# Linear attention and Fourier mixing on one core: keys and own query tiles turned by block transposes on DVE in place of TensorE transposes

## Chip, cores and metric

The kernel runs on one core of one Trainium2 chip. The metric is the device time of one execution in microseconds (us). The engines are named as the profile names them: PE is TensorE, PEld its weight loads, DVE is VectorE, ACT is ScalarE, POOL is GpSimd, SP is SyncE, which issues nearly all DMAs here.

## The reference

Eight batches of 576 tokens, 8 heads of 64 columns (512 columns in all), float32. First a linear attention: softmax of each query over its 64 columns, softmax of each key column over the 576 tokens, a 64x64 product of keys and values for each head, and queries times that product. Then a Fourier mixing over tokens and columns, a layer norm, and two dense layers with a relu between.

```python
q_s = exp(q - max(q, axis=-1));  q_s = q_s / (sum(q_s, axis=-1) + 1e-9)
k_s = exp(k - max(k, axis=2));   k_s = k_s / (sum(k_s, axis=2) + 1e-9)
kv  = einsum('bhsd,bhse->bhde', k_s, v)
x   = einsum('bhsd,bhde->bhse', q_s, kv)          # then laid out as (8, 576, 512)
u   = x + real(fft(fft(x, axis=1), axis=2))
un  = (u - mean(u)) / sqrt(var(u) + 1e-6)         # w_ch1: 512x2048, w_ch2: 2048x512
out = u + relu(un @ w_ch1) @ w_ch2
```

Keys arrive transposed: `kT[b]` is 512 rows (head and column) by 576 tokens. Queries and values arrive as 576 tokens by 512 columns.

## The kernel before

One class, `_Block`, holds all steps as small functions. The main function gives each step a planned time, sorts all steps by it, and issues them in that order; each engine runs its own instructions in the order written. From the second stage on the planned unit is 0.87 us (`scale = 0.87`). So the plan sets only the order on each engine. What sets the real start is the engine itself and its waits.

The work is staged by group of 512 token rows. In stage `order` (1 to 8) PE runs the two dense layers of one group (`up`, 56 units, then `deep_down` or `down`), both as Strassen schemes of seven products over three PSUM banks, `ba`, `bb` and `bc`. The weights stream from HBM in chunks through four places of `big` (`load`, L454); a chunk is asked for when the one four before it is used up (`used`). Between the products of one Strassen step DVE reads a bank and adds a temporary (L1216, L1257 in the up part, L1380 in the down part), and the product after next writes the same bank again.

Into the same stage the attention of batch `b = order + 1` is woven by `attention_timed`, then its folding (`folded`), its Fourier products (`block`, `mix_own`, `mix_shared`) and the norm of the next group. `attention_timed` serves batches 2 to 7. Batch 0 is done in the opening by a list of times written by hand, batch 1 beside the first group's dense layers. Both keep their own steps, of which `first_keys` and the `q_` functions matter here.

For one batch `attention_timed` plans:

- Four key rows `r` (128 rows of `kT`, that is two heads, by 576 tokens). `keys_to` (L642) and `values_to` (L649, L650) load them. `k_exp` takes the maximum along the tokens on DVE (L666), the exponential on ACT with that maximum as its bias and the sum as a second output (L672), and inverts the sum on DVE (L677, L678). `k_turn` transposes four blocks of 128 tokens on PE into PSUM (L690), copies them to SBUF on ACT (L696), then the last block of 128 tokens (L700), of which DVE keeps 64 (L704). `k_times_v` multiplies by the values in five steps (L716) and scales the two diagonal 64x64 blocks by the inverse sum into `kvr` (L724).
- Four own query tiles of 128 tokens. `q_load` (L736) loads one; `q_exp` takes the maximum of each head (L760), eight exponentials of 64 columns with that maximum as bias (L766), sums and inverts on DVE (L785 to L787) and, for two tiles of four, multiplies (L796). `q_turn` transposes four blocks on PE (L824) and copies them out on ACT (L834), for two tiles with the tokens reversed. `q_times_kv` multiplies by `kvr` (L886) and writes the tile, on DVE with the scale (L901) or on ACT without (L903).
- In even batches a tile of tokens shared by two batches, the `t_` functions, which stay on PE.

`ahead(b + 1)` places the first loads of the next batch into the current stage. A float32 product is two PE instructions, each with a weight load; a transpose is one. Waits between engines are set by the tiles that they share: a tile from a pool with n buffers (`bufs=n`) waits for its reader n uses before.

Of the kernel before, what the change touches and what calls it, by code (L numbers as in the profile page):

```python
# [46 lines left out]
P = 128  # L47
B, H, S, DH = 8, 8, 576, 64
D = H * DH
# [11 lines left out]
NT = Q // 2 + 1  # L61
KT = D // P
NF = FF // P
GT = 4 * P
# [72 lines left out]
class _Block:  # L137
    def __init__(self, ctx, tc, q, kT, v, w1, w2, ft, cd, out):
# [14 lines left out]
        for b in range(2):  # L153
            t = c.tile([P, NR, P], F32, name=f"kvr{b}")
            nc.gpsimd.memset(t[:], 0.0)
            self.kvr.append(t)
# [14 lines left out]
        for t in self.kss[:2]:  # L171
            nc.gpsimd.memset(t[0:64, 4, :], 0.0)

# [63 lines left out]
    def warm(self, n):  # L237

        t = self.ps.tile([P, 512], F32, tag="ba", name="ba")
        for _ in range(n):  # L240
            self.nc.tensor.matmul(t[:, 0:2 * P], lhsT=self.ident[:], rhs=self.kvr[1][:, 0:2, :], start=True, stop=True)

# [235 lines left out]
    def attention_timed(self, b, start, end):  # L478

        keys = [("k", b, r) for r in range(NR)]  # L480
        tail = [("t", b)] if b % 2 == 0 else []
        own = [("q", b, c, u) for c, u in ((0, 0), (0, 1), (1, 1), (1, 0))]
        first = start + 14 + 5 * len(tail)
        gap, steps = (end - 13.7 - first) / 3, []
        places = [first + gap * i for i in range(4)]
        shared = start + 14
        if tail and start == 0:
            shared, places = 17, [14, 21, 26, 31.3]
        for i, it in enumerate(keys):
            t = start + 3.5 * i  # L490
            if i > 1:
                steps += at(t - 5, self.k_load(it)[:1]) + at(t + 1.8, self.k_load(it)[1:])
            steps += at(t, self.k_exp(it)) + at(t + 4, self.k_turn(it)) + at(t + 7, self.k_times_v(it))
# [5 lines left out]
        loads = [(t, self.q_load(it)) for t, it in zip(places, own)] + [(shared - 6, self.t_load(it)) for it in tail]  # L499
        loads.sort(key=lambda s: s[0])  # L500
        for t, load in loads[2:]:
            steps += at(t - 6, load)
        return steps + at((33 if start < 0 else 39) if tail else 22, self.t_times_kv(b))

    def ahead(self, b):


        steps = [(20 + r, lambda r=r: self.keys_to(b, r)) for r in range(3)]
        steps += [(35 + r, lambda r=r: self.values_to(b, r)) for r in range(2)]
        q = [self.q_load(("q", b, 0, u)) for u in range(2)]  # L510
# [121 lines left out]

    def k_load(self, it):
        _, b, r = it
        if r < 2:
            return []
        steps = [] if r < 3 else [(0, lambda: self.keys_to(b, r))]
        return (steps or [(0, lambda: None)]) + [(0, lambda: self.values_to(b, r))]

    def keys_to(self, b, r):  # L640
        k = self.work.tile([P, S], F32, tag="k", name="k", bufs=3)[:]
        self.nc.sync.dma_start(k, self.kT[b, r * P:(r + 1) * P, :])  # L642
        self.live["k", b, r] = [k]

    def values_to(self, b, r):
        nc = self.nc
        cols = slice(r * P, (r + 1) * P)
        v = self.work.tile([P, NC, P], F32, tag="v", name="v", bufs=2)
        nc.sync.dma_start(v[:, 0:4, :], self.v[b, 0:512, cols].rearrange("(c p) n -> p c n", p=P))  # L649
        nc.sync.dma_start(v[:, 4, :], self.v[b, S - P:, cols])  # L650
        self.live["k", b, r].insert(1, v)

    def spare(self, n):
# [5 lines left out]
        return t  # L659

    def k_exp(self, it):
        nc, V, live = self.nc, self.nc.vector, self.live

        def top():
            m = self.small.tile([P, 1], F32, tag="km", name="km", bufs=3)
            V.reduce_max(m[:], live[it][0], axis=AX.X, negate=True)  # L666
            live[it].append(m)

        def exp():
            k, m = live[it][0], live[it].pop()  # L670
            rec = self.small.tile([P, 1], F32, tag="krec", name="krec", bufs=8)
            nc.scalar.activation(k, k, ACT.Exp, bias=m[:, 0:1], accum_out=rec[:, 0:1])  # L672
            live[it].append(rec)

        def inverse():
            rec = live[it][2]
            V.tensor_scalar(out=rec[:], in0=rec[:], scalar1=ATT_EPS, scalar2=None, op0=ALU.add)  # L677
            V.reciprocal(rec[:], rec[:])  # L678

        return [(0, top), (0.8, exp), (4.5, inverse)]  # L680

    def k_turn(self, it):
        nc, live = self.nc, self.live
        box = []

        def turn():
            k = live[it][0]
            pt = self.turned()
            for c in range(4):
                nc.tensor.transpose(pt[:, c, :], k[:, c * P:(c + 1) * P], self.ident[:])  # L690
            box.append(pt)

        place = lambda: self.kss[it[2] % 2]

        def four():
            nc.scalar.copy(place()[:, 0:4, :], box.pop(0)[:])  # L696

        def last():
            pt = self.turned()
            nc.tensor.transpose(pt[:, 0, :], live[it][0][:, S - P:], self.ident[:])  # L700
            box.append(pt)

        def fifth():
            nc.vector.tensor_copy(place()[64:, 4, :], box.pop(0)[64:, 0, :])  # L704
            live[it].append(place())

        return [(0, turn), (0.7, four), (0.7, last), (1.2, fifth)]

    def k_times_v(self, it):
        nc, live, (_, b, r) = self.nc, self.live, it  # L710

        def times():
            _, v, rec, ks = live.pop(it)
            pk = self.acc((P, P))
            for c in range(NC):
                nc.tensor.matmul(pk, lhsT=ks[:, c, :], rhs=v[:, c, :], start=(c == 0), stop=(c == NC - 1))  # L716
            live[it] = pk, rec

        def scale():
            pk, rec = live.pop(it)  # L720
            for h in range(2):
                s = slice(64 * h, 64 * h + 64)
                to = self.kvr[b % 2][s, r, s]
                nc.vector.tensor_scalar(out=to, in0=pk[s, s], scalar1=rec[s, 0:1], scalar2=None, op0=ALU.mult)  # L724

        return [(0, times), (1.7, scale)]

# [99 lines left out]
    def q_turn(self, it):  # L827
        _, b, c, u = it
        box = []

        def copy():
            pt = box.pop()
            qT = self.work.tile([P, NR, P], F32, tag="qT", name="qT", bufs=2)
            self.nc.scalar.copy(qT[:], pt[:] if c == u else pt[:, :, ::-1])  # L834
            self.live[it][0] = qT

        return [(0, lambda: box.append(self.turned_q(it))), (0.8, copy)]
# [31 lines left out]
    def q_times_kv(self, it):  # L869
# [10 lines left out]
        def times():  # L880
            qT, *rec = self.live.pop(it)
            px = self.acc((P, D))
            box.insert(0, px)
            box.extend(rec)
            for r in range(NR):
                nc.tensor.matmul(px[:, r * P:(r + 1) * P], lhsT=qT[:, r, :], rhs=self.kvr[b % 2][:, r, :], start=True,  # L886
                                 stop=True)
# [19 lines left out]
    def t_times_kv(self, b):  # L907
# [5 lines left out]
        def times():  # L913
            px = self.acc((P, D))
            for r in range(NR):
                nc.tensor.matmul(px[:, r * P:(r + 1) * P], lhsT=self.F[:, 2 * r + j], rhs=kvr[:, r, :], start=True,
                                 stop=True)
            box.append(px)
# [617 lines left out]
def kernel(ctx: ExitStack, tc: tile.TileContext, q, kT, v, w1, w2, ft,  # L1536
# [149 lines left out]
```

## Time and profile before

| what | value |
|---|---|
| median of 3 runs | 1069.19 us (1068.7 to 1069.22) |
| span of the profiled execution | 1068.4 us, 16964 instructions |
| PE granted clock, mean | 1.000 |
| DMA | 236.04 MB, mean 221 GB/s |
| PE key transposes, L690 and L700 | x96 and x24, 273 ns each |
| PE query transposes, L824 from `q` | x124, 273 ns each |
| PE key products, L716 | x240, 275 ns each |
| ACT query exponentials, L766 | x216, 338 ns each |
| stage of batch 4 (529 to 644 us): PE, DVE, ACT, POOL busy | 115.0, 74.8, 43.1, 52.3 us |

The span runs from the first to the last instruction of one profiled execution; the time of a run takes in what lies around it. No separate time is recorded for the profiled execution. PE's instructions are pipelined, so the 273 ns of one are longer than the distance to the next. A group's line gives the engine, the operation, output and inputs by tile, the shape, the count, the busy time and the mean time of one; then the idle time of the engine before them and what ended it. A line of the order of time gives start and length in us.

### The profile page before, as it was taken

To read this page: it belongs to the slowest core of one execution; us is meant where nothing else is said; L and a number is where in the kernel's file an instruction comes from. 1 tells how busy PE (TensorE), PEld (TensorE's weight loads), DVE (VectorE), ACT (ScalarE), POOL (GpSimd) and SP (SyncE) were. 2 spreads that over 40 slices of the span, in tenths; PEclk is the share of its full clock that TensorE was granted. 3 is DMA by queue.
4 is the path that set the end of the run, shared out by engine and by line. 5 is a ranking of instruction groups with operands and counts; after the bars stand their busy time and mean duration, and the time that the engine had idled before them with its cause. 6 is when DMAs were issued, how large, how long until landed. Compare 5 with 4: busy or idle time off the path is not lost.

```text
span 1068.4 us, 16964 instructions
## 1 busy us (share of the span) xinstructions
PE 1056.4 (99%) x6394; PEld 920.5 (86%) x6394; DVE 698.9 (65%) x1350; ACT 398.2 (37%) x925; POOL 380.4 (36%) x321
## 2 busy tenths in 40 slices
PE   8999999999999999999999999999999999999998
PEld 7744556988898899889998999889988998899898
DVE  6898887675455785677555765678457654674563
ACT  5674433642245215631443234521552132231210
POOL 3263320265511734454515542384336350000000
PEclk9999999999999999999999999999999999999999
DMA  8687578648976576646755576557644575576464
GB/s 266 237 294 251 179 244 294 205 156 284 331 257 207 195 254 235 226 165 209 262 192 193 197 242 213 198 200 257 223 168 158 198 253 181 194 260 221 173 215 151
DMA packets 113546, 236.04 MB, mean 221 GB/s; under 512 B 23272, under 2 KB 74856, under 8 KB 102840
## 3 DMA queue, kind: packets, MB, share of 16 engines
q1 hardware_dynamic: 113096, 234.42, 64.3%
q8 instruction: 51, 0.84, 0.3%
q10 hardware_dynamic: 288, 0.26, 0.1%
q14 instruction: 31, 0.25, 0.1%
q0 software_dynamic: 80, 0.26, 0.1%
HBM read 199.79 MB, written 39.06 MB: 224 GB/s over the span
## 4 chain that ended last, share of the span: by engine, by line
PE 88%; DVE 1%; ACT 1%; issue 0%; POOL 0%; ACTq 0%
PE bb L1246 16%; PE bc L1246 10%; PE ba L1246 10%; PE bb L1373 10%; PE bc L1373 7%; PE ba L1373 7%; PE bb L1343 5%; PE acc L716 3%; PE acc L886 2%; PE bc L1183 2%; PE bb L1462 2%; PE acc L999 2%; PE acc L1002 2%; PE acc L1027 2%; PE bc L1462 1%; PE ba L1462 1%
## 5 line engine op out<-in xcount | busy, mean ns | idle before, releaser
L1246 PE MATMUL bb<-unT,big 128*128 128x256 f32 x768 | 184.2, 379 | 0.0
L1246 PEld LDWEIGHTS bb<-unT,big 128*128 128x128 f32 x768 | 142.7, 190 | 18.7 <-DVE u L1216 0.6
L1258 ACT ACTIVATE big<-big 128x512 f32<-128x512 f32 x96 | 60.4, 629 | 195.7 <-DVE big L1257 195.3
L1246 PE MATMUL ba<-unT,big 128*128 128x256 f32 x512 | 123.8, 379 | 0.0
L1246 PE MATMUL bc<-unT,big 128*128 128x256 f32 x512 | 123.4, 379 | 0.0
L1216 DVE TENSOR_TENSOR u<-bb,s 128x512 f32<-128x512 f32 x66 | 45.5, 689 | 104.8 <-PE bb L1246 84.6
L383 POOL TENSOR_TENSOR big<-big 128x512 f32<-128x512 f32 x24 | 30.5, 1269 | 224.6 <-ACT big L1258 224.6
L1246 PEld LDWEIGHTS bc<-unT,big 128*128 128x128 f32 x512 | 94.7, 190 | 12.4 <-DVE big L1257 0.8
L1373 PE MATMUL bb<-big 128*128 128x128 f32 x848 | 105.1, 275 | 0.3 <-DVE u L1380 0.3
L1246 PEld LDWEIGHTS ba<-unT,big 128*128 128x128 f32 x512 | 94.4, 190 | 12.2 <-issue 0.5
L1373 PEld LDWEIGHTS bb<-big 128*128 128x128 f32 x848 | 99.6, 192 | 0.5 <-DVE u L1380 0.4
L1323 POOL TENSOR_TENSOR x<-x,big 128x512 f32<-128x512 f32 x45 | 57.7, 1296 | 62.1 <-issue 32.3
L1373 PE MATMUL ba<-big 128*128 128x128 f32 x640 | 79.6, 275 | 0.0
L1373 PEld LDWEIGHTS ba<-big 128*128 128x128 f32 x640 | 76.3, 192 | 1.2
L1319 DVE TENSOR_TENSOR big<-big 128x512 f32<-128x512 f32 x98 | 75.3, 806 | 0.0
L766 ACT ACTIVATE q<-q,qm 128x64 f32<-128x64 f32 x216 | 58.5, 338 | 25.4 <-DVE qm L760 18.9
L1380 DVE TENSOR_TENSOR u<-bb,s 128x256 f32<-128x256 f32 x40 | 16.8, 421 | 65.0 <-PE bb L1373 61.6
L1343 PE MATMUL bb<-big 128*128 128x256 f32 x256 | 58.7, 381 | 0.0
L1257 DVE TENSOR_TENSOR big<-bc,u 128x512 f32<-128x512 f32 x64 | 43.9, 686 | 21.8 <-PE bc L1246 21.0
L1122 POOL TENSOR_TENSOR unT<-unT 128x512 f32<-128x512 f32 x8 | 14.2, 1771 | 123.4 <-DVE unT L1122 100.8
L1343 PEld LDWEIGHTS bb<-big 128*128 128x128 f32 x256 | 48.2, 190 | 8.0 <-DVE big L1257 1.1
L1373 PE MATMUL bc<-big 128*128 128x128 f32 x416 | 51.5, 275 | 0.0
(268 smaller groups left out, 2028.4 us busy)
## 6 DMA issues: line engine op xcount, KB each, us to landing
big<-w2d SPq DMA_DIRECT2D x67, 1024.0 KB, 4.8
big<-w1s SPq DMA_DIRECT2D x64, 896.0 KB, 4.8
big<-w2s SPq DMA_DIRECT2D x16, 1024.0 KB, 6.6
big<-in_w_dram SPq DMA_DIRECT2D x21, 512.0 KB, 6.2
w2d<-big SPq DMA_DIRECT2D x42, 256.0 KB, 5.4
q<-in_q_dram SPq DMA_DIRECT2D x28, 256.0 KB, 6.6
k<-in_kT_dram SPq DMA_DIRECT2D x24, 288.0 KB, 5.5
v<-in_v_dram SPq DMA_DIRECT2D x24, 256.0 KB, 4.5
```

Of the source, the lines that this page charges most:

```text
L383: e1.tensor_tensor(out=to(4), in0=at(2), in1=at(3), op=ALU.add)
L716: nc.tensor.matmul(pk, lhsT=ks[:, c, :], rhs=v[:, c, :], start=(c == 0), stop=(c == NC - 1))
L766: nc.scalar.activation(q[:, h, :], q[:, h, :], ACT.Exp, bias=m[:, h:h + 1])
L1216: plus = lambda t: V.tensor_tensor(out=temp(t), in0=box["bb"][:], in1=box["s1"][:], op=ALU.add)
L1246: nc.tensor.matmul(bank()[:, i, :], lhsT=w[:, WA_AT[m], k * P:(k + 1) * P], rhs=self.unT[g][:, B_AT[m], k, :], start=first and i == 0 and ...
L1257: steps = [(0, lambda: V.tensor_tensor(out=hp(i), in0=bank()[:], in1=u()[:], op=ALU.add)), (0.8, lambda: nc.scalar.activation(hp(i), hp(i) ...
L1258: (0.8, lambda: nc.scalar.activation(hp(i), hp(i), ACT.Relu))]
L1319: e.tensor_tensor(out=to(o), in0=to(x), in1=to(y), op=op)
L1323: E.tensor_tensor(out=x, in0=x, in1=tile(m), op=ALU.add)
L1343: nc.tensor.matmul(box[name][:, i, :], lhsT=h[p][:, A_AT[m], i * P:(i + 1) * P], rhs=self.stream[n][:, p, :], start=p == 0 and (m != 1 or ...
L1373: nc.tensor.matmul(box[place[n]][:, i, :], lhsT=own(m)(A_AT[n])[:, f, :], rhs=w[:, r // 2, r % 2 * P:r % 2 * P + P], start=first and f == ...
L1462: nc.tensor.matmul(bank()[:, i, :], lhsT=h[p][:, A_AT[m], i * P:(i + 1) * P], rhs=w[:, p, :], start=first and i == 0 and p == 0, stop=p == ...
```

## The change

For batches 2 to 7 the 128x128 transposes on PE give way to 32x32 block transposes on DVE, in place.

Keys: `kb` is one tile of 128 partitions by 16 groups of 160 tokens. Partition quarter `i` holds 160 tokens of the sequence, group `g` holds 32 of the 512 key rows, one row to a partition. The last quarter overlaps the third, as 576 is less than 640. The maximum over all tokens is then taken along the 160, and between the four quarters by copies on ACT and minima of negated maxima on DVE (`across`). ACT takes 16 exponentials of 128x160. A block transpose turns each 32 rows by 32 tokens, the tokens being every fifth one; the products read the turned keys in steps of five elements, five products to a key row as before. The values are loaded so that token and partition agree, with zeros where tokens overlap, and carry a column of ones, so that the product's column 128 is the sum.

Queries: POOL subtracts the maximum (`less`), DVE transposes the 16 blocks of the tile in place, ACT takes 16 exponentials of 32x128 that also move each block to its partition quarter, and `kvr` carries two columns of ones, so that the products give the sums of the two heads beside them. The output is scaled on DVE for all four tiles. The planned times of the steps, the loads ahead of them and the number of buffers change with it; `ks` of the opening lies in `kb`.

```diff
-            t = c.tile([P, NR, P], F32, name=f"kvr{b}")
+            t = c.tile([P, NR, P + 2], F32, name=f"kvr{b}")
...
-        self.kss = [c.tile([P, NC, P], F32, name=f"ks{i}") for i in range(2)]
-        self.kss += [self.work.tile([P, NC, P], F32, tag="v", name="ks", bufs=2) for _ in range(2)]
+        self.kb = c.tile([P, 4 * NR, Q, NC], F32, name="kb")
+        kb = self.kb[:].rearrange("p g s c -> p (g s c)")
+        self.kss = [kb[:, i * NC * P:(i + 1) * NC * P].rearrange("p (c n) -> p c n", n=P) for i in range(NR)]
+        self.vt = [c.tile([P, NC, P + 1], F32, name=f"vt{i}") for i in range(2)]
...
     def attention_timed(self, b, start, end):
+        places, shared = [6, 13.5, 21.5, 27.2], start + 12
+        if tail:
+            places = [8.5, 14, 21.5, 27.2]
+        if start == 0:
+            places, shared = [13.5, 20.5, 24, 27.2], 7
+        steps = at(start, self.keys(b))
...
         for t, it in zip(places, own):
-            steps += at(t, self.q_exp(it)) + at(t + 8.7, self.q_turn(it)) + at(t + 12.1, self.q_times_kv(it))
+            steps += at(t, self.own_exp(it)) + at(t + 15, self.own_times_kv(it))
...
     def ahead(self, b):
+        steps = at(24 if b > 2 else 20, self.keys_to(b))
+        for r in range(2):
+            steps += at((35 if b > 2 else 51) + r, self.values_to(b, r))
...
+    def keys_to(self, b):
+        def load(i):
+            rows = self.kT[b].rearrange("(g p) s -> p g s", p=Q)
+            a = min(i * NC * Q, S - NC * Q)
+            self.nc.sync.dma_start(self.kb[i * Q:i * Q + Q].rearrange("p g s c -> p g (s c)"), rows[:, :, a:a + NC * Q])
+        return [(0.6 * i, lambda i=i: load(i)) for i in range(4)]
...
     def values_to(self, b, r):
+            load(t[0:3 * Q, :, 0:P], v[0:full].rearrange("(p c) n -> p c n", c=NC))
+            load(t[n:, :, 0:P], v[S - (P - n) * NC:].rearrange("(p c) n -> p c n", c=NC))
+            load(t[VZ:n, NC - 1, 0:P], v[full:full + 1])
...
+    def prepare(self):
+        G = self.nc.gpsimd
+        for t in self.kvr:
+            for h in range(2):
+                G.memset(t[64 * h:64 * h + 64, :, P + h:P + h + 1], 1.0)
+        for t in self.vt:
+            G.memset(t[3 * Q:], 0.0)
+            G.memset(t[:, :, P:P + 1], 1.0)
...
+    def keys(self, b):
+        def top(r):
...
+            V.reduce_max(box["m"][:, 4 * r:4 * r + 4], kb[:, 4 * r:4 * r + 4].rearrange("p g s c -> p g (s c)"), axis=AX.X, negate=True)
+        def exp(g):
+            k = kb[:, g].rearrange("p s c -> p (s c)")
+            nc.scalar.activation(k, k, ACT.Exp, bias=box["m"][:, g:g + 1])
+        def turn(r):
+            t = kb[:, 4 * r:4 * r + 4].rearrange("p g s c -> p g c s")
+            V.transpose(t, t)
+        def times(r):
+            pk = box[r] = self.acc((P, P + 1))
+            for c in range(NC):
+                nc.tensor.matmul(pk, lhsT=kb[:, 4 * r:4 * r + 4, :, c].rearrange("p g s -> p (g s)"),
+                                 rhs=self.vt[r % 2][:, c, :], start=c == 0, stop=c == NC - 1)
...
+        steps = [(0.9 * r, lambda r=r: top(r)) for r in range(NR)]
+        steps += at(3.6, self.across(lambda: box["m"], 2, 4 * NR)) + at(4.5, self.across(lambda: box["m"], 1, 4 * NR))
+        steps += [(6 + g / 2, lambda g=g: exp(g)) for g in range(4 * NR)]
+        for r in range(NR):
+            for dt, f in ((8.3, turn), (10.8, times), (12.5, scale)):
+                steps.append((dt + 2 * r + 4 * (r > 1 and f != turn), lambda f=f, r=r: f(r)))
+        steps += at(11.5, self.values_to(b, 2)) + at(13.5, self.values_to(b, 3))
...
+    def own_exp(self, it):
+        def less():
+            G.tensor_tensor(out=heads(), in0=heads(), in1=m[:].unsqueeze(2).to_broadcast([P, H, DH]), op=ALU.add)
+        def turn():
+            V.transpose(live[it][0], live[it][0])
...
+        def exps(some):
+            of, to = (t.rearrange("p (r i n) -> i p r n", r=NR, i=4) for t in live[it])
+            for n in some:
+                i, t = n // 4, n % 4
+                one = of[i, t * Q:t * Q + Q]
...
+                nc.scalar.activation(to[t, i * Q:i * Q + Q], one, ACT.Exp)
...
+        return [(0, top), (0.9, less), (2.7, turn)] + [(3.6 + n / 2, lambda n=n: exps((n, n + 1))) for n in range(0, 16, 2)]
+    def own_times_kv(self, it):
+        def times():
...
+                px = self.acc((P, 2 * (P + 2))).rearrange("p (r n) -> p r n", r=2)
+                    nc.tensor.matmul(px[:, r, :], lhsT=q[:, 2 * half + r, :], rhs=self.kvr[b % 2][:, 2 * half + r, :],
+                                     start=True, stop=True)
+        def inverse():
...
+                V.tensor_scalar(out=rec[:, half], in0=box[half][:, :, P:], scalar1=ATT_EPS, scalar2=None, op0=ALU.add)
...
+        return [(0, times), (1.5, inverse), (1.6, lambda: out(0)), (1.7, lambda: out(1))]
...
-    def k_exp(self, it):
-    def k_turn(self, it):
-    def k_times_v(self, it):
...
+    steps.append((first + 60, blk.prepare))
```

More of the change, by code (lines that the diff above doesn't have):

```diff
@@ L240, in warm @@
         for _ in range(n):
-            self.nc.tensor.matmul(t[:, 0:2 * P], lhsT=self.ident[:], rhs=self.kvr[1][:, 0:2, :], start=True, stop=True)
+            self.nc.tensor.matmul(t[:, 0:2 * P], lhsT=self.ident[:], rhs=self.kvr[1][:, 0:2, 0:P], start=True, stop=True)
     def halves(self):
@@ L497, in attention_timed @@
         for t, it in zip(places, own):
-            steps += at(t, self.q_exp(it)) + at(t + 8.7, self.q_turn(it)) + at(t + 12.1, self.q_times_kv(it))
-        loads = [(t, self.q_load(it)) for t, it in zip(places, own)] + [(shared - 6, self.t_load(it)) for it in tail]
+            steps += at(t, self.own_exp(it)) + at(t + 15, self.own_times_kv(it))
+        loads = [(t - 7, t + 7.6, self.own_load(it)) for t, it in zip(places, own)]
+        loads += [(shared - 13, shared + 8.4, self.t_load(it)) for it in tail]
         loads.sort(key=lambda s: s[0])
-        for t, load in loads[2:]:
-            steps += at(t - 6, load)
-        return steps + at((33 if start < 0 else 39) if tail else 22, self.t_times_kv(b))
+        free = [-99] * 3
+        for i, (t, end, load) in enumerate(loads):
+            if i > 1:
+                steps += at(max(t, free[-3]), load)
+            free.append(end)
+        return steps + at((33 if start < 0 else 39) if tail else max(22, start + 24), self.t_times_kv(b))
     def ahead(self, b):
-        steps = [(20 + r, lambda r=r: self.keys_to(b, r)) for r in range(3)]
-        steps += [(35 + r, lambda r=r: self.values_to(b, r)) for r in range(2)]
-        q = [self.q_load(("q", b, 0, u)) for u in range(2)]
+        steps = at(24 if b > 2 else 20, self.keys_to(b))
+        for r in range(2):
+            steps += at((35 if b > 2 else 51) + r, self.values_to(b, r))
+        q = [self.own_load(("q", b, 0, u)) for u in range(2)]
         if b % 2 == 0:
@@ new lines, in values_to, with load @@
+    def values_to(self, b, r):
+        def load():
+            t, cols = self.vt[r % 2], slice(r * P, (r + 1) * P)
+            v = self.v[b, :, cols]
+            full, n = 3 * Q * NC, VZ + 1
+            load = self.nc.sync.dma_start
+            load(t[0:3 * Q, :, 0:P], v[0:full].rearrange("(p c) n -> p c n", c=NC))
+            load(t[n:, :, 0:P], v[S - (P - n) * NC:].rearrange("(p c) n -> p c n", c=NC))
+            load(t[VZ:n, NC - 1, 0:P], v[full:full + 1])
+        return [(0, load)]
@@ new lines, in across, with copies, least @@
+    def across(self, box, by, n):
+        nc = self.nc
+        other = []
+        def copies():
+            m = box()
+            w = self.small.tile([P, n], F32, tag="across", name="across", bufs=2)
+            other.append(w)
+            if by == 2:
+                for h in range(2):
+                    nc.scalar.copy(w[64 * h:64 * h + 64], m[64 - 64 * h:128 - 64 * h])
+            else:
+                for i in range(4):
+                    nc.scalar.copy(w[i * Q:i * Q + Q], m[(i ^ 1) * Q:(i ^ 1) * Q + Q])
+        def least():
+            m = box()
+            nc.vector.tensor_tensor(out=m[:], in0=m[:], in1=other.pop()[:], op=ALU.min)
+        return [(0, copies), (0.3 + 0.15 * (4 // by), least)]
@@ L659, in spare @@
         return t
-    def k_exp(self, it):
[L662 to L680, printed above, removed]
-    def k_turn(self, it):
[L683 to L707, printed above, removed]
-    def k_times_v(self, it):
[L710 to L726, printed above, removed]
     def q_load(self, it):
@@ L832, in copy @@
             pt = box.pop()
-            qT = self.work.tile([P, NR, P], F32, tag="qT", name="qT", bufs=2)
-            self.nc.scalar.copy(qT[:], pt[:] if c == u else pt[:, :, ::-1])
+            qT = self.work.tile([P, D], F32, tag="qT", name="qT", bufs=3)[:].rearrange("p (r n) -> p r n", n=P)
+            self.nc.scalar.copy(qT, pt[:] if c == u else pt[:, :, ::-1])
             self.live[it][0] = qT
```

84 lines of the change are left out of this document (53 added, 31 removed).

## The prediction

> **What bounds the kernel now.** I read the page's totals first, then what PE waited for, then the order of time around one batch's attention, then the groups by shape.
>
> ```profile
> PE 1056.4 (99%) x6394; PEld 920.5 (86%) x6394; DVE 698.9 (65%) x1350; ACT 398.2 (37%) x925; POOL 380.4 (36%) x321
> ...
> PEclk9999999999999999999999999999999999999999
> ```
>
> PE is busy for all but 12 us of the 1068.4 us span, at full granted clock; DVE has a third of the span free, ACT and POOL almost two thirds. A busy share alone proves little, so the second view is the list of PE's waits:
>
> ```profile
> PE ba L241 <- POOL kvr L155: 2.3, 1, 2.3
> PE acc L999 <- issue: 1.7, 1, 1.7
> PE tr L537 <- ACT big L532: 1.3, 2, 0.9
> ...
> PE acc L886 <- ACT qT L834: 0.3, 1, 0.3
> PE bb L1373 <- DVE u L1380: 0.3, 1, 0.3
> ```
>
> The longest belong to the opening. In the stages of batches 2 to 7 almost nothing makes PE wait, so an instruction taken from PE there is time off the end, as long as no new wait takes its place. Third, PE in order of time at the attention of one batch:
>
> ```profile
> 526.38 0.60 PE L690 MATMUL tr<-ident,k 128*128 128x128 f32 x4
> 526.82 0.27 PE L700 MATMUL tr<-ident,k 128*128 128x128 f32 x1
> 526.92 1.95 PE L1373 MATMUL bc<-big 128*128 128x128 f32 x16
> ...
> 529.58 1.28 PE L716 MATMUL acc<-v,ks 128*128 128x128 f32 x10
> 530.69 0.60 PE L690 MATMUL tr<-ident,k 128*128 128x128 f32 x4
> ...
> 548.64 0.60 PE L824 MATMUL tr<-ident,q 128*128 128x128 f32 x4
> 549.08 1.89 PE L1246 MATMUL bb<-unT,big 128*128 128x256 f32 x8
> ```
>
> Starts, not lengths, give the price, since lengths overlap: four transposes move the next start by 0.44 us, a fifth by 0.10, ten products of 128 columns by 1.11 (0.111 each), eight of 256 columns by 1.73 (0.216 each).
>
> **Removed from PE.** Per batch, 4 key rows with 5 transposes (L690, L700) and 4 own tiles with 4 (L824), which is 36, and 216 in six batches. By the starts that is 4 x (0.44 + 0.10) + 4 x 0.44 = 3.92 us a batch, 23.5 us in all. The instruction lists of the two kernels differ on PE by just these 216.
>
> **Added to PE.** The column of ones makes 240 key products 129 columns wide and two columns make 192 query products 130. A column costs (0.216 - 0.111) / 128 = 0.8 ns, so 240 x 0.8 + 192 x 1.6 ns = 0.5 us. Net -23.0 us.
>
> The stationary operand of those 240 key products is now read in steps of five elements (20 bytes). No PE row of this trace reads in steps. The nearest rows:
>
> ```profile
> L716 PEld LDWEIGHTS acc<-v,ks 128*128 128x128 f32 x240 | 30.6, 192 | 1.2
> L1036 ACT COPY sn<-acc 128x256 f32<-128x256 f32 x20 | 7.5, 375 | 27.6 <-PE acc L1027 23.4 <-issue 4.2
> L1387 ACT COPY s<-ba 128x256 f32<-128x256 f32 x20 | 7.4, 372 | 47.8 <-PE ba L1373 47.8
> ```
>
> A load lasts 192 ns while a pair goes by every 111, so at most 111 ns of it cannot be hidden. Lower bound of the extra cost: 0. Upper bound: that part doubles, 240 x 0.111 = 26.6 us. L1036 reads 256 columns from two halves in turn, 512 bytes apart, and takes 375 ns against 372 for the plain copy of L1387. It is another engine and PSUM, so it is weak support, but it is the only row of long steps; I take 0 and keep the other end.
>
> [...]
>
> **DVE.** Off per batch: 4 key maxima of 745 ns, 4 x (144 + 164) key inverses, 4 copies of the fifth block at 294, 4 sums of queries at 681, 4 x (408 + 203) inverses, 2 products at 692, 2 outputs at 681: 13.3 us. On: 4 maxima over 640 elements (663 ns for 512, 745 for 576, so 0.83 us), 2 small minima (0.15), key inverses 1.3, query inverses 4 x (2 x 0.17 + 0.20), 8 outputs of 128x256 at 0.42 (L1380): 10.5 us. The block transposes are in no row. Lower bound: a pass at the rate of a 128x512 reduction (0.66; 0.83 for 640 elements), 4 x 0.83 + 4 x 0.66 = 6 us; upper bound: twice that, 12. I take 8, since the query tiles lie densely and the key tiles in steps. So DVE gets about +5 us a batch (+3 to +9). It lies beside PE's products:
>
> ```profile
> 529.00:590.00 61.00, 61.00 (x338) 54.59 (x337) 35.80 (x71) 26.79 (x67) 25.56 (x21) 1.00 0.61 203
> ```
>
> The columns after the length are PE, PEld, DVE, ACT, POOL. DVE goes from 35.8 of 61 us to some 41 of 57: still room, but its instructions run in the order written, and PE's Strassen chain waits for it:
>
> ```profile
> 579.03 1.89 PE L1246 MATMUL bb<-unT,big 128*128 128x256 f32 x8
> 580.76 1.89 PE L1246 MATMUL bc<-unT,big 128*128 128x256 f32 x8
> 582.49 1.89 PE L1246 MATMUL bb<-unT,big 128*128 128x256 f32 x8
> ```
>
> and, on DVE in the same stretch:
>
> ```profile
> 581.02 0.69 DVE L1216 TENSOR_TENSOR u<-bb,s 128x512 f32<-128x512 f32 x1 [3.71 <-PE bb L1246]
> ```
>
> Bank bb is done at about 580.9, DVE reads it until 581.71 and PE writes it again at 582.49: 0.78 us of slack. A transpose of 0.8 us that has just started ahead of L1216 fits; one of 1.3 us is 0.5 too long. The same holds for a DVE instruction that itself waits (a transpose for POOL's subtraction, the inverse for the products). Bounds: 0, and 0.5 us for each of 48 transposes, 24 us. I take 0.35 us a batch, 2 us: the list of PE's waits above shows how rarely the present strings (a 0.69 sum, two small ones and a 0.69 product at L785 to L796) break that slack.
>
> **ACT.** Off: 4 x (774 + 188 + 581) for keys, 32 x 338 for query heads, 4 x 578 and 2 x 581 for copies: 20.5 us. On: 16 exponentials of 128x160 (338 ns at 64 elements and 774 at 576 give 0.85 ns an element, so 420 ns), 64 of 32x128 without a bias (630 ns at 512, so 304), 6 small copies at 0.19: 27.4. That is +7 us a batch, 26.8 to 34 of 57 us in the window above. A tile's 16 exponentials are 4.9 us in 8 planned units of 0.87 us (7 us), and its products are planned 3.4 units after the last pair: nothing on the path, and if that cover were gone the cost is the DVE stall's kind, 1 to 2 us a tile.
>
> **POOL and queues.** The subtraction of the maximum comes to POOL, 24 x 1.12 us (L812), in the gaps between its four sums of 1.27 a Strassen step; 10 one-time fills stand ahead of conversions that PE needs some 10 us later. Per batch SP issues 4 key loads of a quarter of the partitions and 12 value pieces instead of 4 and 8, at 0.3 to 0.5 us an issue, +2 us of its time. Behind them wait the weight chunks; these are asked for three chunks ahead (18 us in the up part), so a 2 us delay is hidden. The keys now have one buffer: their next loads stand 3 planned units or more behind the last key product that frees it. I count nothing for either.
>
> **Sum.** 1068.4 - 23.5 + 0.5 + 2 = 1047.4 us of span. The median of the runs is 0.8 us above this span, so 1048.2, say 1048.
>
> **Rivals.**
> 1. Steps in the weight load. The 240 key loads no longer hide behind products. From a pair pitch of 0.111 + 23.0 / 240 = 0.207 us on, the whole gain is gone. At twice the unhidden part: 1048.2 + 26.6 = 1075, slower by 0.5%. For it: loads are 86% of the span, so PE is as near to load-bound as to product-bound. Against it: L1036. [...] A penalty of half that size gives 1061.
> 2. DVE in order. Transposes near the upper bound, and waits for POOL at the head of DVE's queue, let L1216 and the sums after it come late: 24 us at most, 10 us as a middle, 1058. For it: 0.78 us of slack. Against it: 48 transposes do not all fall ahead of L1216.
> 3. ACT or SP late: PE waits for exponentials or a weight chunk at each tile, 24 x 1 us, which is 1072. Against it: 3.4 units of planned slack and 18 us of chunks.
>
> **Chances.** Forecast (1044 to 1053) 0.62; rival 2 (1053 to 1066) 0.13; rival 1 at half price (1056 to 1066) 0.05 and at full price (1067 to 1082) 0.13; rival 3 and anything else 0.07, mostly above 1067. No change can be told within about 0.2%, 2 us, so same means 1067 to 1071. Faster: 0.62 + 0.13 + 0.05 - 0.04 for tails = 0.76; same 0.06; slower 0.18. The range reaches from all transposes gained with no new stall and a little more (1044) to where rival 1 takes almost all of it back (1069).
>
> **What would show it.** Right: PE has 216 fewer transposes, its waits for DVE and ACT in the stages of batches 2 to 7 come to a few us, ten key products still move the next start by 1.1 us, each stage between two batches is 3.5 us shorter. Rival 1: ten key products take 2 us or more and the loads of kb are longer than 192 ns. Rival 2: transposes of more than 1.2 us, PE bb waiting for DVE u. Rival 3: query products waiting for ACT qT, or chunks for DMA. I am wrong as soon as a stage is not at least 2 us shorter.

## The result, and the profile after

The changed kernel takes 1085.81 us (median of 4 runs, 1084.55 to 1087.37) against 1069.2 (1068.7 to 1069.39) for the kernel before: a ratio of 1.0154, 95% interval 1.0139 to 1.0168. It is slower by 1.5%; 1048 was predicted, and the range ended at 1069. The span of the profiled execution is 1082.8 us, its time 1084.55.

The page's totals after (engine, busy time, share, instructions) and the granted clock in 40 slices:

```profile
PE 1062.8 (98%) x6178; PEld 925.8 (85%) x6178; DVE 735.1 (68%) x1410; ACT 456.7 (42%) x1141; POOL 407.8 (38%) x353
...
PEclk9999999999999999999999999999999999999999
```

PE issues the 216 instructions fewer that were forecast, and yet it is busy 6.4 us longer than before. So most of the loss is not waiting: some of PE's own instructions have become slower. The order of time on PE, at the second key row of batch 5, shows which:

```profile
548.17 2.27 PE L715 MATMUL acc<-vt,kb 128*128 128x129 f32 x10
550.27 1.89 PE L1334 MATMUL bb<-unT,big 128*128 128x256 f32 x8
```

The ten products move PE's next start by 2.10 us, where they moved it by 1.11 before. The groups by shape (count, then busy us and mean ns of one, then idle time before them and its releaser) give the loads behind it, and the new instructions on DVE and ACT:

```profile
L774 ACT ACTIVATE qT<-q 32x128 f32<-32x128 f32 x384 | 117.9, 307 | 13.2 <-DVE q L764 8.1
...
L715 PEld LDWEIGHTS acc<-vt,kb 128*128 128x128 f32 x240 | 54.9, 313 | 4.6 <-DVE kb L710 4.0
...
L710 DVE STREAM_TRANSPOSE kb<-kb 128x640 f32<-128x640 f32 x24 | 33.4, 1392 | 7.2 <-ACT kb L706 7.2
...
L764 DVE STREAM_TRANSPOSE q<-q 128x512 f32<-128x512 f32 x24 | 17.0, 708 | 3.6 <-POOL q L761 2.9
```

A key load lasts 313 ns instead of 192. The second part of the loss is in the list of PE's waits:

```profile
PE bb L1334 <- DVE km L689: 4.2, 1, 4.2
...
PE acc L715 <- DVE kb L710: 2.0, 5, 0.5
...
PE bb L1334 <- DVE u L1304: 1.3, 2, 0.8
```

One single wait of 4.2 us stands out. The others in the stages of batches 2 to 7 are at most 0.8 us each, but 5.0 us in all, where 2 were forecast. The long one lies at the start of batch 2's stage. PE there, in order of time:

```profile
179.64 1.93 PE L1334 MATMUL bc<-unT,big 128*128 128x256 f32 x8
185.82 3.75 PE L1334 MATMUL bb<-unT,big 128*128 128x256 f32 x8 [4.25 <-DVE km L689]
189.36 3.04 PE L1334 MATMUL ba<-unT,big 128*128 128x256 f32 x8
```

The eight products at 185.82 move the next start by 3.54 us and the next eight by 2.88, where 1.73 is usual. The same stretch in windows (length, busy time and count of PE, PEld, DVE, ACT, POOL, then granted clock, DMA share, GB/s) says why:

```profile
182.00:184.00 2.00, 0.00 (x0) 0.00 (x0) 0.42 (x1) 0.00 (x0) 0.00 (x0) 1.00 1.19 334
184.00:186.00 2.00, 0.18 (x1) 0.21 (x2) 0.77 (x2) 1.20 (x4) 0.00 (x0) 0.71 0.82 213
186.00:188.00 2.00, 2.00 (x5) 1.64 (x6) 0.77 (x2) 1.73 (x7) 0.00 (x0) 0.50 0.88 339
```

All engines stand still from 182.4 to 184.1 us, the transfers are full (a share of 1.19), and PE is granted half its clock from 184.9 to 191.7 us (0.93 in the window from 184 to 185, 0.50 up to 191, 0.66 from there to 192), which takes in its first 5.9 us of work after the pause. The releaser that is named, the small minimum `km` at L689, only stands just behind the real one on DVE, the sum `u` at L1304, which reads bank `bb`. DVE's and ACT's own lines say what held the work up:

```profile
184.13 0.58 ACT L1305 COPY s<-ba 128x512 f32<-128x512 f32 x1 [16.60 <-DMA w2s<-s]
184.98 0.69 DVE L1304 TENSOR_TENSOR u<-bb,s 128x512 f32<-128x512 f32 x1 [2.56 <-DMA w2s<-u]
```

ACT may not write the temporary `s` again, nor DVE `u`, before the old content has been stored (L437). SP's queue, in order of time, shows what stands ahead of these stores:

```profile
156.29 0.72 SPq L650 DMA_DIRECT2D vt<-in_v_dram  x1
...
160.15 2.22 SPq L652 DMA_DIRECT2D vt<-in_v_dram  x1
...
180.75 0.59 SPq L437 DMA_DIRECT2D w2s<-s  x1
181.43 0.69 SPq L437 DMA_DIRECT2D w2s<-u  x1
```

Between 156.3 and 162.4 us SP issues the six value pieces of batch 2, which the kernel before loads from 139.7 us on; the two stores come at 180.75 and 181.43, in the kernel before at 176.22 and 176.77.

By stage, from the first `up` product of one group to that of the next (us; the columns are named by the batch whose attention lies in the stage):

| kernel | 2 | 3 | 4 | 5 | 6 | 7 |
|---|---|---|---|---|---|---|
| before | 119.18 | 116.60 | 115.26 | 115.83 | 115.26 | 115.71 |
| after | 128.92 | 118.93 | 116.01 | 116.71 | 116.02 | 117.15 |
| after less before | +9.74 | +2.33 | +0.75 | +0.88 | +0.76 | +1.44 |

By these starts the stretch from 529 to 644 us, which the table ahead of the prediction calls the stage of batch 4, is that of batch 5.

Two readings are to be tested: a constant price in all six stages (the slow products: 40 x 0.099 = 3.96 us a stage, 23.8 in all, which eats the 3.83 that the transposes should give), and a stall in the first of them.

### The profile page after: what moved, and what is told of

It reads as the page before. It is cut to its first block, busy times and chain, and to the rows that moved or that the text cites. A ratio compares the mean times of both kernels' runs of the same rounds, so it can differ in the third digit from the quotient of the medians.

```text
span 1082.8 us, 16800 instructions
## 1 busy us (share of the span) xinstructions
PE 1062.8 (98%) x6178; PEld 925.8 (85%) x6178; DVE 735.1 (68%) x1410; ACT 456.7 (42%) x1141; POOL 407.8 (38%) x353
## 4 chain that ended last, share of the span: by engine, by line
PE 85%; DVE 5%; ACT 4%; DMA 4%; SPq 1%; issue 1%; POOL 0%; ACTq 0%; DVEq 0%; POOLq 0%
PE bb L1334 13%; PE bc L1334 9%; PE bb L1461 9%; PE ba L1334 8%; PE ba L1461 6%; PE bc L1461 6%; PE bb L1431 5%; PE acc L715 5%; ACT qT L774 2%; PE bb L1550 2%; PE acc L790 2%; PE bb L1250 2%; PE acc L1087 2%; PE ba L1250 2%; PE bc L1250 2%; PE acc L1090 2%
## 5 line engine op out<-in xcount | busy, mean ns | idle before, releaser
L1334 PEld LDWEIGHTS bb<-unT,big 128*128 128x128 f32 x768 | 145.4, 192 | 26.4 <-issue 4.8
L774 ACT ACTIVATE qT<-q 32x128 f32<-32x128 f32 x384 | 117.9, 307 | 13.2 <-DVE q L764 8.1
L1304 DVE TENSOR_TENSOR u<-bb,s 128x512 f32<-128x512 f32 x66 | 45.5, 689 | 98.8 <-PE bb L1334 81.0
L1461 PEld LDWEIGHTS bb<-big 128*128 128x128 f32 x848 | 99.6, 192 | 0.5 <-DVE u L1468 0.5
L761 POOL TENSOR_TENSOR q<-q,qm 128x512 f32<-128x512 f32 x24 | 25.8, 1073 | 144.1 <-DVE qm L756 108.4
L715 PEld LDWEIGHTS acc<-vt,kb 128*128 128x128 f32 x240 | 54.9, 313 | 4.6 <-DVE kb L710 4.0
L715 PE MATMUL acc<-vt,kb 128*128 128x129 f32 x240 | 55.8, 379 | 2.0 <-DVE kb L710 2.0
```

The source lines that it names most:

```text
L715: nc.tensor.matmul(pk, lhsT=kb[:, 4 * r:4 * r + 4, :, c].rearrange("p g s -> p (g s)"), rhs=self.vt[r % 2][:, c, :], start=c == 0, stop=c ...
L761: G.tensor_tensor(out=heads(), in0=heads(), in1=m[:].unsqueeze(2).to_broadcast([P, H, DH]), op=ALU.add)
L774: nc.scalar.activation(to[t, i * Q:i * Q + Q], one, ACT.Exp)
L1304: plus = lambda t: V.tensor_tensor(out=temp(t), in0=box["bb"][:], in1=box["s1"][:], op=ALU.add)
L1334: nc.tensor.matmul(bank()[:, i, :], lhsT=w[:, WA_AT[m], k * P:(k + 1) * P], rhs=self.unT[g][:, B_AT[m], k, :], start=first and i == 0 and ...
L1461: nc.tensor.matmul(box[place[n]][:, i, :], lhsT=own(m)(A_AT[n])[:, f, :], rhs=w[:, r // 2, r % 2 * P:r % 2 * P + P], start=first and f == ...
```

## The experiments

Main theory: the weight loads that read `kb` in steps of 20 bytes cost 0.099 us a product. Rivals: the new work on DVE and ACT makes PE wait; the queries' half gives nothing. Side theory: the stall of batch 2 comes from SP's queue and full transfers. All kernels, for reference (us, ratio to the kernel before on the same chip with its 95% interval, and three of the stages):

| kernel | median | ratio | stage 2 | 3 | 4 |
|---|---|---|---|---|---|
| after | 1085.81 | 1.0154 (1.0139 to 1.0168) | 128.92 | 118.93 | 116.01 |
| e1_dense | 1064.26 | 0.9953 (0.9936 to 0.9971) | 126.83 | 116.19 | 112.11 |
| e2_early | 1083.21 | 1.0131 (1.0114 to 1.0148) | 122.01 | 118.96 | 116.03 |
| e3_step5 | 1083.46 | 1.0131 (1.0114 to 1.0148) | 121.17 | 118.59 | 117.24 |
| e4_step24 | 1082.57, one run | | 121.01 | 118.42 | 117.09 |
| e5_both | 1061.10 | 0.9931 (0.9913 to 0.9949) | 119.91 | 116.75 | 112.14 |
| e6_idle | 1058.68 | 0.9902 (0.9886 to 0.9919) | 120.46 | 116.53 | 112.14 |
| e7_queries | 1093.09 | 1.0230 (1.0210 to 1.0251) | 124.57 | 119.26 | 119.52 |
| e8_keys | 1067.20 | 0.9990 (0.9978 to 1.0001) | 121.16 | 117.24 | 113.88 |
| e10_later | 1056.36 | 0.9886 (0.9869 to 0.9903) | 119.38 | 114.62 | 112.14 |

### e1_dense: the block transposes write densely

The changed kernel, but the block transpose of a key row is no longer in place: it reads `kb` in steps and writes a dense tile in a free part of `big`. The products load from there without steps.

```diff
-            V.transpose(t, t)
+            V.transpose(kt(r).rearrange("p c g s -> p g c s"), t)
...
-                nc.tensor.matmul(pk, lhsT=kb[:, 4 * r:4 * r + 4, :, c].rearrange("p g s -> p (g s)"),
+                nc.tensor.matmul(pk, lhsT=kt(r)[:, c].rearrange("p g s -> p (g s)"),
```

> The changed kernel, but the block transposes of the keys write to a second place in which the 128 columns of each weight load lie side by side; tokens, loads and order of the work stay. Theory (weight loads in steps of 20 bytes): ten key products move the next start by 1.11 us again in place of 2.10, 240 x 0.099 = 24 us come back, 1085.8 - 24 = 1062 us. Rival (PE is held by late DVE and ACT work, the loads are only seen waiting): the products may be quicker, but the time stays above 1078.

Measured: 1064.26. This one edit turns 1.5% slower into 0.5% faster. PE in order of time, then the groups of PE's key loads and DVE's transposes:

```profile
544.81 1.28 PE L719 MATMUL acc<-vt,big 128*128 128x129 f32 x10
545.93 1.89 PE L1338 MATMUL bc<-unT,big 128*128 128x256 f32 x8
```

```profile
L719 PEld LDWEIGHTS acc<-vt,big 128*128 128x128 f32 x240 | 29.8, 191 | 8.1 <-DVE big L714 4.1 <-issue 3.1
L714 DVE STREAM_TRANSPOSE big<-kb 128x640 f32<-128x640 f32 x24 | 32.4, 1348 | 7.1 <-ACT kb L710 7.1
```

The ten products move the next start by 1.12 us again, and a load lasts 191 ns. DVE's transpose still reads in steps and still takes 1348 ns, so it is not DVE's time that had gone onto the path but PE's loads. The stage of batch 4 falls from 116.01 to 112.11, by 3.90 of the 3.96 worked out above. In the stages of batches 2 and 3 only 2.09 and 2.74 come back, in part because PE there now waits 1.2 us each for values.

### e3_step5: the steps alone, in the kernel before

The kernel before, in which only the transposed keys of rows 1 and 3 are stored with steps of five elements. ACT's and DVE's copies write these steps, and the helper that does it splits ACT's copy for rows 0 and 2 into four of 128x128; ACT's exponentials, the loads and the plan are untouched.

```diff
+KSTEP = (1, 5)
...
+    def kpart(self, i, c):
+        if i > 1:
+            return self.kss[i][:, c, :]
+        m, t = KSTEP[i], self.kss[i]
+        at = c // m * m
+        n = min(m, NC - at)
+        return t[:, at * P:(at + n) * P].rearrange("p (n a) -> p a n", a=n)[:, c - at, :]
...
-                nc.tensor.matmul(pk, lhsT=ks[:, c, :], rhs=v[:, c, :], start=(c == 0), stop=(c == NC - 1))
+                nc.tensor.matmul(pk, lhsT=self.kpart(ks, c), rhs=v[:, c, :], start=(c == 0), stop=(c == NC - 1))
```

> The kernel before, nothing turned on DVE; only the copy of the turned keys of rows 1 and 3 (buffer 1) is written so that the weight loads read it in steps of five elements. Theory: the products of these 12 rows in batches 2 to 7 take 2.1 us for ten instead of 1.11, 12 x 0.99 = 12 us, and up to 1.6 us in the opening: 1081 to 1083 us, with rows 0 and 2 at 1.11 us beside them. Rival (steps cost nothing by themselves): 1069 us.

Measured: 1083.46, just above the expected 1081 to 1083, and stages 2.0 us longer, as the main theory has it. Two rows at 0.99 us more make up these 2.0, which leaves nothing for ACT's longer copies (1097 ns for 128x512 in steps, 581 dense). PE, a row in steps:

```profile
551.96 2.27 PE L735 MATMUL acc<-v,ks 128*128 128x128 f32 x10
554.07 1.03 PE L1265 MATMUL bb<-unT,big 128*128 128x256 f32 x4
```

The start moves by 2.11 us; the row before it, stored densely, moves it by 1.11. Taking the steps out of the changed kernel and putting them into the old one show the same price.

### e4_step24: which steps cost

The same kernel with steps of two elements in rows 0 and 2, and of four in the first four chunks of rows 1 and 3.

```diff
-KSTEP = (1, 5)
+KSTEP = (2, 4)
```

> The kernel before, with the transposed keys of rows 0 and 2 stored in steps of two elements (8 bytes) and the first four chunks of rows 1 and 3 in steps of four elements (16 bytes); the fifth chunk of rows 1 and 3 stays dense. Read from the distance between PE's next start and the start of each row's ten key products: dense is 1.11 us, steps of five elements gave 2.10. [...] Rival: any step costs, in proportion to the bytes spanned; then rows 0 and 2 already rise by about 0.25 us and rows 1 and 3 by 0.6. Time by the first: 1069 + 12 x 0.8 = 1079.

Measured, a row of two-element steps and a row of four-element steps on PE:

```profile
546.82 1.32 PE L735 MATMUL acc<-v,ks 128*128 128x128 f32 x10
547.98 0.60 PE L709 MATMUL tr<-ident,k 128*128 128x128 f32 x4
...
551.12 2.15 PE L735 MATMUL acc<-v,ks 128*128 128x128 f32 x10
553.10 1.03 PE L1265 MATMUL bb<-unT,big 128*128 128x256 f32 x4
```

The ten products move the next start by 1.16 us and 1.98. Eight of ten are stepped in each, so a step of 8 bytes costs 0.05 / 8 = 0.006 us a product, one of 16 bytes 0.87 / 8 = 0.109, about as much as one of 20 (0.099). The price does not grow with the bytes spanned, it jumps between 8 and 16 bytes. The rival of a price in proportion falls. The 1079 expected charges 8 x 0.099 = 0.8 us to each of 12 rows of four-element steps and nothing to the two-element ones; measured are 0.87 and 0.05 us a row. The time of 1082.57 is above it: the six stages are 11.0 us longer (9.6 expected), and the opening, which reads stepped rows too and was not counted, 1.5.

### e2_early, e5_both, e6_idle: the stall in batch 2's stage

e2_early is the changed kernel with batch 2's first values at planned unit 35 instead of 51, so that SP has issued them before the stores of `s` and `u`. e5_both is the same with dense keys.

```diff
-            steps += at((35 if b > 2 else 51) + r, self.values_to(b, r))
+            steps += at(35 + r, self.values_to(b, r))
```

> The changed kernel, with the first value loads of batch 2 at planned unit 35 in place of 51, ahead of the stores of the combined weights on SP instead of among them. Theory (six more DMAs push the last stores, which hold the temporaries s1 and u2, late): PE's 4.2 us wait at the first Strassen step of batch 2's stage goes, and with it the low granted clock after it, about 3 us: 1085.8 - 7 = 1079 us. Rival (the wait comes from the four key maxima on DVE, or the stores are late anyway): 1085 to 1086 us.

> Both edits of the two kernels before it. If the two costs are separate they add: 1085.8 - 24 - 7 = 1055 us, 1.3% under the kernel before. If the PE time that comes back turns into waits for DVE and ACT: above 1062 us.

Measured in e2_early: 1083.21, of the 7 us expected only 2.6. The wait of 4.2 us is gone and the stage of batch 2 is 6.9 us shorter, but it begins 5.3 us later. The longest wait of PE is now in the norm just before it:

```profile
PE tr L1195 <- ACT eo L1189: 2.5, 1, 2.5
```

e5_both has these values at the same places: DVE is busy there for 0.55 us of the six from 148 to 154 us, in e1_dense, with the later places, for 4.43. So the standstill moved to an earlier stretch; what DVE waits for in it is not shown. e5_both, 1061.10, beats both kernels but misses the 1055 expected, and keeps that wait (2.4 us). e6_idle, with dense keys, therefore loads keys and values where SP and the transfers were idle:

```diff
-        steps = at(24 if b > 2 else 20, self.keys_to(b))
+        steps = at(24 if b > 2 else 5, self.keys_to(b))
...
-            steps += at((35 if b > 2 else 51) + r, self.values_to(b, r))
+            steps += at((35 if b > 2 else 9) + r, self.values_to(b, r))
```

> The changed kernel with dense key tiles, and batch 2's key loads moved from planned unit 20 to 5 and its first two value loads from unit 51 to 9 and 10, where SP and the transfers had idle time. If what is left of the loss in the stages of batch 1 and 2 is the queue of SP (the late stores of s and u in one placing, the late norm in the other), both waits go and the time is about 1061 - 5 = 1056 us. Rival: the transfers are short in bandwidth over the whole opening, the wait only moves a third time, and the time stays at 1061 or more.

Measured: 1058.68, between the two expectations; its interval overlaps e5_both's. Neither wait is left. What PE still waits for, in that kernel's list:

```profile
PE acc L719 <- DMA vt<-in_v_dram: 3.0, 2, 1.6
```

These are the values of row 3 in the stages of batches 2 and 3. That the two big waits came from the place of these loads in SP's order is shown, since placing alone removed them. Whether it is SP's time to issue them or the full transfers that make the stores late is not separated, nor is it shown that no further wait hangs on bandwidth.

### e7_queries and e8_keys: which half pays

e7_queries is the kernel before with the queries' half of the change alone. It has two `qT` buffers where the changed kernel has three, and its products are planned 11.8 units after the tile's start, where the changed kernel has 15.

```diff
-            steps += at(t, self.q_exp(it)) + at(t + 8.7, self.q_turn(it)) + at(t + 12.1, self.q_times_kv(it))
+            steps += at(t, self.own_exp(it)) + at(t + 11.8, self.own_times_kv(it))
```

> The kernel before with only the own query tiles of batches 2 to 7 turned on DVE and their sums from columns of ones; keys, their loads and their transposes on TensorE stay as before. If the stepped weight loads of the keys (and the new loads of keys and values in batch 2's stage) make the whole loss, this half alone gains its 96 transposes: 24 x 0.44 = 10.6 us less 0.3 for wider columns, about 1059 us, and each stage is some 1.7 us shorter. Rival: DVE's and ACT's new work costs PE about as much as the transposes did; then the time is 1066 or more and waits of query products for ACT qT or of PE bb for DVE u show some 10 us.

Measured: 1093.09, the slowest of all. Its list of waits:

```profile
PE acc L719 <- ACT qT L703: 22.5, 16, 2.7
```

By its numbers the rival holds. But 16 exponentials alone take 16 x 0.32 = 5.1 us on ACT, and 11.8 units less the 3.6 before the first exponential leave 7.1 us for them and all else on ACT. So the run does not tell whether the work or my place for it is at fault. e8_keys asks it the other way round: e6_idle with the queries back on PE, at the places of the kernel before.

```diff
-            steps += at(t, self.own_exp(it)) + at(t + 15, self.own_times_kv(it))
+            steps += at(t, self.q_exp(it)) + at(t + 8.7, self.q_turn(it)) + at(t + 12.1, self.q_times_kv(it))
```

> Like e6_idle (dense key tiles, batch 2's loads early), but the own query tiles go through TensorE again as in the kernel before: 24 x 4 transposes and the separate sums of queries are back, while the keys stay on DVE. If both halves of the change pay what their transposes cost on PE, the queries' half is worth 24 x 0.44 = 10.6 us less 0.3, and this kernel takes 1058.7 + 10 = 1069, stages of batches 4 to 7 some 1.7 us longer than in e6_idle. Rival, to which e7_queries points: the queries' half gives its gain back in waits for ACT's exponentials; then this kernel takes 1060 or less.

Measured: 1067.20, and 113.88 us for the stage of batch 4, 1.74 longer than in e6_idle. So at the places of the changed kernel the queries' half is worth 8.5 us of the 10.3 worked out: 1.7 in each of the stages of batches 4 to 7, 0.7 in those of batches 2 and 3. The 22.5 us of e7_queries then belong to its places or its buffers, which of the two is not separated. The keys' half alone, even with dense loads, gains 1.38 us in the stage of batch 4 (115.26 - 113.88) and gives 1.98 and 0.64 back in those of batches 2 and 3; the ratio of 0.9990 can't be told from no change.

### e9_later and e10_later: can the last waits be planned away

> Like e6_idle, with the key products planned one unit (0.87 us) later, and for rows 2 and 3 of batches 2 and 3 two more. If the idle time of PE that is left in those stages (3.4 and 3.1 us in batches 2 and 3, 0.5 in each later one: waits for the values of rows 2 and 3 and for the block transposes) is only a matter of planned places, about 5 us of it goes and the time is near 1054. Rival: the waits follow the products, since transfers and DVE's order set them; then the time stays within 2 us of e6_idle.

In e9_later the planned places put the products of rows 0 and 1 behind the loads of the values of rows 2 and 3 into the same two buffers, so they multiply by those; its 1109.89 us answer another question. e10_later keeps within the bound. Besides the line shown, it plans the products of the tile of shared tokens three units later (`start + 27` for `start + 24`):

```diff
-                steps.append((dt + 2 * r + 4 * (r > 1 and f != turn), lambda f=f, r=r: f(r)))
+                steps.append((dt + 2 * r + 4 * (r > 1 and f != turn) + (0.6 if r == 0 else late * (r == 3)) * (f != turn), lambda f=f, r=r: f(r)))
```

> Like e6_idle, with the product of key row 0 planned 0.6 units (0.52 us) later in every batch, and that of row 3 of batches 2 and 3 two units (1.74 us) later. PE in e6_idle waits 1.62 and 1.41 us for the values of row 3 there and 0.2 to 0.5 us for the block transpose of row 0 in each of six batches. If these waits are only a matter of planned places, 3 + 2 = 5 us of idle time goes and the time is about 1054. Rival: the waits follow the products, since what sets them is the order on SP and DVE behind earlier products; then the time stays within 2 us of 1058.7.

Measured: 1056.36, 2.3 below e6_idle, with overlapping intervals. The waits for the values and the block transposes are gone from the list, and another has taken their place:

```profile
PE bb L1338 <- DVE u L1308: 6.5, 6, 2.1
```

The stages of batches 2 and 3 are 1.1 and 1.9 us shorter than in e6_idle, that of batch 4 is the same, 112.14. So for the values the places mattered; for the block transposes the wait only moved: in the stages of batches 4 to 7 PE now waits 0.74 to 0.82 us for a sum `u`, which in e6_idle's order on DVE stands right behind a key transpose of 1.37 us (419.23, the sum at 420.51). At a ratio of 0.9886 (0.9869 to 0.9903) it is the fastest measured, with an interval that overlaps e6_idle's, and 1.1% faster than the kernel before.

## Why the prediction was wrong

**The step that failed.** "I take 0 and keep the other end", for the weight loads in steps of five elements. They cost 240 x 0.099 = 23.8 us, close to the upper bound of 26.6. That bound rested on the right row (a load of 192 ns in a pitch of 111) and on a doubling that no row supported; by luck it came nearly true: 0.111 became 0.210. The value chosen rested on ACT reads of PSUM, in single elements taken from two halves in turn. They cost 375 ns against 372 at a distance of 512 bytes, but on another engine and from another memory, which says nothing about PE's loads of elements 20 bytes apart in SBUF. Where PE's loads were 86% busy, a step on the load side should have been taken from the upper end. Rival 1 at its full price gave 1075 and had 0.13, and it was the one that held: the loads of `kb` last 313 ns and ten key products move the next start by 2.10 us.

**The second step that failed.** "A 2 us delay is hidden", and "I count nothing for either", of SP's queue. This looked at the weight chunks in the up part, for which no PE wait shows, and not at what stands behind the six value pieces ahead of batch 2's stage: the stores of `s` and `u`, for which ACT and DVE wait. The 2 us were mis-sized as well: "0.3 to 0.5 us an issue" for 12 value pieces. By the trace SP is busy with issues for 337.1 us in all, 264.2 before, which is 12 a batch. Of the 337.1, 59.2 us are the third piece of each value load (L652), one token of 128 columns:

```profile
221.13 8.42 SPq L652 DMA_DIRECT2D vt<-in_v_dram  x1
```

This is the longest of the 24; their mean is 2.47 us. Why so small a piece keeps SP so long is not shown. The stage of batch 2 is 9.6 us longer than loads and transposes account for, that of batch 3 2.2, while the stage of batch 2 begins 1.5 us earlier.

**The account.** Of the span: -23.5 + 0.5 as forecast, + 23.8 for the loads, + 9.6 + 2.2 - 1.5 for the stages of batches 2 and 3 and the start, and + 3.3 in the other four stages (0.6, 0.75, 0.6 and 1.3, from the table of stages less 0.13 each): 14.4, which is 1082.8 - 1068.4. The loads and the stages of batches 2 and 3 together make 34.1 of the 35.4 us between forecast and result. The first part is shown; of the second, 10.3 us, placing the loads elsewhere gives back 5.6 (e1_dense to e6_idle), and the rest is not traced to one cause.

**What held.** The transposes on PE: in e6_idle the stage of batch 4 is 3.12 us shorter with 0.49 us of waits in it, so 3.6 of 3.83 are there. The block transposes: 4 x 1.39 + 4 x 0.71 = 8.4 us a batch, taken as 8. The exponentials: 416 and 307 ns, estimated as 420 and 304. ACT as a whole grew more, (456.7 - 398.2) / 6 = 9.8 us a batch instead of 7, and DVE (735.1 - 698.9) / 6 = 6.0 instead of 5; in the changed kernel both stayed beside PE's work.

**Rivals 2 and 3.** In the changed kernel PE waits 1.3 us for DVE's `u` and 1.0 for ACT's `qT`: neither decided. Both kinds of wait exist, though: e10_later shows the first, with 6.5 us for `u`; e7_queries shows the second with 22.5. The 2 us for all stalls were too little: without the loads' price and the big wait, the stages of e6_idle still lie 0.7 to 1.5 us above what the transposes and columns alone would give in batches 4 to 7, and 5.1 and 3.8 in batches 2 and 3. How much of these last is bandwidth and how much place stays open.

## What to carry to other kernels

A layout that spares an engine an instruction moves a step to whoever reads the result; when that reader is PE's weight load with no time to spare (here 192 ns became 313), ask for its price by a row of the same engine and memory, or take the upper bound. Let the engine that has time (here DVE's transpose, 1348 ns in e1_dense against 1392 in place) do the stepped access and write densely. Where loads are moved in a full queue, look at every store behind them and at who waits for it, in the first stage apart from the steady ones.

## What was not expected of the hardware

- A pause can cost more than its length. In e7_queries pauses of PE up to 2.06 us left the granted clock at 1.00, two of 2.35 us once left it and once did not, and after those of 2.61 to 2.72 us it fell to 0.50 for 3.4 us. Length alone does not decide: in e8_keys the products behind a pause of 2.99 us keep their usual pace (four move the next start by 0.86 us), and that run's mean clock is 1.000.
- Steps cost other engines too: in e3_step5 ACT's copy of 128x512 into steps of 20 bytes took 1097 ns against 581 dense in the kernel before. DVE's block transpose took 1392 ns in the changed kernel for 640 stepped elements against 708 for 512 dense, 1.6 times the time for each element; no run has a dense one of 640.
- Exponentials on 32 partitions follow each other at 0.32 us, with no overlap (ten in 3.20 us in e7_queries), where six of 128x64 take 1.54 us in e8_keys (0.26 each). So the estimate of 304 ns for each new one was near what they fill. The removed ones were overcounted: 338 ns is the duration of one, but the 216 of the kernel before fill 58.5 us, 0.27 each. For 32 a batch that is 2.1 of the 2.8 us by which ACT grew more than forecast.
